# Weight blocks of a two-layer feed-forward stage run ahead by a fifth part, end behind the next functions, and come in another order

## The chip, the cores and the metric

The kernel runs on one NeuronCore of one Trainium2 chip. The metric is the device time of one launch in microseconds (us), the median of several runs. Engines: PE (TensorE, matrix multiply), DVE (VectorE), ACT (ScalarE), POOL (GpSimd), SP (SyncE, which only issues DMAs here).

## The reference, cut to what matters

```
x = attention(q, k, v)                 # 2 x 8 heads, 576 positions, head size 64, with rotary embedding
x = x.reshape(1152, 512)
h = x @ w1_in                          # 512 -> 2048
x = elu(h) @ w1_out                    # 2048 -> 512
h = x @ w2_in                          # 512 -> 2048
out = (h * tanh(softplus(h))) @ w2_out # mish, 2048 -> 512
```

The weights reach the chip as 64-bit floats. Each product is made of three passes on numbers that are split into a high and a low part (hi·hi, hi·lo, lo·hi).

## The kernel before, in words

**Blocks of weights.** Each of the four weight matrices is cut into 16 blocks of 128x512. One block is a *job*: SP loads `raw` (512 KB); POOL makes `wu` from the upper words (L96); DVE adjusts exponent, sign and mantissa in three instructions (L100, L104, L108); and the last step is two instructions, ACT copying `wu` to the high part (L122) and POOL subtracting it to get the low part (L123). `weight_stages` is a generator that yields between these parts. `open_job` starts a job (load and L96), `advance` runs its next part, `weight_part` opens jobs until two run and advances the older, `weight_job` runs parts until one more job is finished. After the opening part a job has four parts: three on DVE and the last step. Tiles are named by matrix side and parity of the group of four blocks: `wi0h`, `wi0l`, `wi1h`, ..., `wo1l`; each name has four buffers.

**The list of jobs.** Jobs 0 to 31 are the first layer's blocks (w1_in and w1_out by turns, in groups of four). Jobs 32 to 63 are the second layer's. Groups 4 to 7 name its four groups. Before, jobs 32 to 47 are: w2_in group 4, w2_in group 5, w2_out group 4, w2_out group 5.

**Steps.** Behind the attention come 64 steps. Step n makes one first product (`g1_mm`, L183: 24 matmuls of 288 columns into a PSUM tile `ps_s`), applies the function to it, issues second products that have become due, and takes up some weight work. Steps 0 to 31 are the first layer: `elu` (ACT L214, L215, L216; DVE L217, L218), `elu_hi` (ACT L223), `elu_lo` (DVE L227), second products `g2_first` (L624: 24 matmuls into `ps_g`). In steps 4 to 30 four weight parts, one job, go into each step: three ahead of `elu`, one behind it. Steps 32 to 63 are the second layer: `mish_a` (ACT L580 tanh and L581 silu straight from `ps_s`, DVE L582), and in batches of two or four steps `mish_b` (ACT L588, after a table load), `mish_c` (ACT L594, after another table load, DVE L595) and `mish_d` (ACT L601, DVE L602); second products `g2_second` (L653: 12 matmuls of 512 columns into `ps_h`), whose first sums into `Y` ACT copies (L657) and whose later ones DVE adds (L659). From step 31 on, each step ends with one `weight_job`, step 36 with two. Of the first layer's last group, four `g2_first` are put off to steps 34, 35, 36 and 38; their results become `XH` (ACT L638) and `XL` (DVE L639).

**What sets the order.** In the first half every engine runs its instructions in the order in which the code writes them. In the second half only ACT does; for the other engines a scheduler decides when the program is built. On the chip each engine runs its own list strictly in order, so an instruction that waits holds back everything behind it on that engine.

**Which step reads what.** Steps 32 to 35 and 40 to 43 read w2_in group 4, steps 36 to 39 and 44 to 47 group 5. The first `g2_second` is due at step 39 and reads w2_out group 4.

Of the kernel before, what the change touches and what calls it, by code (L numbers as in the profile page):

```python
# [13 lines left out]
AF = mybir.ActivationFunctionType  # L14
# [13 lines left out]
def kernel(  # L28
# [11 lines left out]
    nc = tc.nc  # L40
# [10 lines left out]
    GF = 4  # L51
    GB, GE, PB = 9, 2, 5
    NG = NF // GF
# [32 lines left out]
    def weight_stages(key):  # L86
        kind, c = key
        raw = raws.pop(key)
        if wide:


            w = raw.rearrange("p (n w) -> p n w", w=2)
            low, high = w[:, :, 0], w[:, :, 1]
            u = wpool.tile([128, 512], F32, tag="wu", name="wu", bufs=2)
            ui = u.bitcast(I32)
            nc.gpsimd.tensor_scalar(  # L96
                out=u, in0=high.bitcast(F32), scalar1=REBASE, scalar2=0.0, op0=ALU.mult, op1=ALU.add
            )
            yield
            nc.vector.tensor_scalar(  # L100
                out=ui, in0=ui, scalar1=3, scalar2=0x7FFFFFF8, op0=ALU.logical_shift_left, op1=ALU.bitwise_and
            )
            yield
            nc.vector.scalar_tensor_tensor(  # L104
                out=ui, in0=high, scalar=-0x80000000, in1=ui, op0=ALU.bitwise_and, op1=ALU.bitwise_or
            )
            yield
            nc.vector.scalar_tensor_tensor(  # L108
                out=ui, in0=low, scalar=29, in1=ui, op0=ALU.logical_shift_right, op1=ALU.bitwise_or
            )  # L110
            yield
        else:
            u = raw
        even = c // GF % 2 == 0
        pool, tag = wpool if even else late_pool[0], ("wi", "wo")[kind] + ("0" if even else "1")
        hi = pool.tile([128, 512], F32R, tag=tag + "h", name=tag + "h", bufs=GF)
        lo = pool.tile([128, 512], F32R, tag=tag + "l", name=tag + "l", bufs=GF)
        if kind == 0:
            WI[c] = (hi.rearrange("p (c f) -> p c f", c=NC), lo.rearrange("p (c f) -> p c f", c=NC))
        else:  # L120
            WO[c] = (hi, lo)
        nc.scalar.activation(out=hi, in_=u, func=AF.Copy)  # L122
        nc.gpsimd.tensor_tensor(out=lo, in0=u, in1=plain(hi), op=ALU.subtract)  # L123

    jobs = []
    for kind, g in [(k, g) for g in range(NG) for k in range(2)] + [
        (0, NG), (0, NG + 1), (1, NG), (1, NG + 1), (0, NG + 2), (0, NG + 3), (1, NG + 2), (1, NG + 3)
    ]:
        jobs += [(kind, g * GF + i) for i in range(GF)]
    loaded, opened, njob = [0], [0], [0]  # L130
    running = []

    def prefetch_weights(n):
        while loaded[0] < min(len(jobs), opened[0] + n):
            load_weight(jobs[loaded[0]])
            loaded[0] += 1

    def open_job():
        prefetch_weights(3)
        running.append(weight_stages(jobs[opened[0]]))  # L140
        opened[0] += 1
        advance(-1)
        prefetch_weights(3)

    def advance(i):
        if next(running[i], True):
            running.pop(i)
            njob[0] += 1

    def weight_part():  # L150
        while len(running) < 2 and opened[0] < len(jobs):
            open_job()
        if running:
            advance(0)

    def weight_job():
        n = min(njob[0] + 1, len(jobs))
        while njob[0] < n:
            weight_part()
# [35 lines left out]
    def tmp(tag):  # L195
        if tmp_pool[0] is not None:
            return tmp_pool[0].tile([128, S], F32, tag="P", name="P", bufs=PB)
        return late_pool[0].tile([128, S], F32, tag=tag, name=tag, bufs=5)
# [363 lines left out]
    def moe(mp, early):  # L562
# [15 lines left out]
        def mish_a(n, m, f, b, o):  # L578
            t, s = tmp("ta"), tmp("tb")
            nc.scalar.activation(out=v2(t), in_=o[:, :, :HS], func=AF.Tanh, scale=0.5)  # L580
            nc.scalar.activation(out=v2(s), in_=o[:, :, :HS], func=AF.Silu)  # L581
            nc.vector.scalar_tensor_tensor(out=s, in0=t, scalar=-3.0, in1=s, op0=ALU.add, op1=ALU.mult)  # L582
            mst[n] = (m, f, b, t, s)
# [6 lines left out]
        def mish_c(ns):  # L590
            nc.scalar.preload_act_table_set("silu_and_others")
            for n in ns:
                m, f, b, t, s = mst[n]
                nc.scalar.activation(out=t, in_=t, func=AF.Tanh, scale=-1.0)  # L594
                nc.vector.scalar_tensor_tensor(out=s, in0=t, scalar=1.0, in1=s, op0=ALU.add, op1=ALU.mult)  # L595

        def mish_d(ns):
            for n in ns:
                m, f, b, t, s = mst.pop(n)
                gh, gl = galloc(m, f, b)  # L600
                nc.scalar.activation(out=gh, in_=s, func=AF.Copy, scale=-0.25)  # L601
                nc.vector.scalar_tensor_tensor(  # L602
                    out=gl, in0=s, scalar=-0.25, in1=plain(gh), op0=ALU.mult, op1=ALU.subtract
                )
                seam(m, f, b)
# [35 lines left out]
        def g2_second(g, t):  # L641
            o = g_pool[0].tile([128, 512], F32, tag="h", name="ps_h", bufs=2)
            b, s0 = divmod(t * 128, S)
            k = 0
            for fi in range(GF):
                f = NF + g * GF + fi
                hi, lo = WO[f]
                if s0 + 128 <= S:
                    gh, gl = (G[f, b][:, i, s0:s0 + 128] for i in range(2))
                else:  # L650
                    gh, gl = (GX[f][:, i, :] for i in range(2))
                for l, w in ((gh, hi), (gl, hi), (gh, lo)):
                    nc.tensor.matmul(o, lhsT=l, rhs=w, start=(k == 0), stop=(k == 3 * GF - 1))  # L653
                    k += 1
            y = get_y().rearrange("p (t e) -> p t e", e=DM)[:, t, :]
            if g == 0:
                nc.scalar.activation(out=y, in_=o, func=AF.Copy)  # L657
            else:
                nc.vector.tensor_tensor(out=y, in0=y, in1=o, op=ALU.add)  # L659
                if g == NG - 1:  # L660
                    nc.sync.dma_start(out=out[t * 128:t * 128 + 128, :], in_=y)
# [4 lines left out]
        blocks[-4:] = [(1, g, b) for g in range(NG - 2, NG) for b in range(NB)]  # L666
        g1_seq = [(m, g * GF + fi, b) for m, g, b in blocks for fi in range(GF)]
        half = len(g1_seq) // 2
        D1, D2, LATE, XJ = 1, 4, (3, 4, 5, 7), 4
        pend = []  # L670

        def run_g2(it):
# [10 lines left out]
        def step(n, late):  # L683
            m, f, b = g1_seq[n]
            o = early.pop(n) if n in early else g1_mm(m, f, b)
            if late:
                mish_c(late)
            done, late = late, []
            if m == 0:
                for _ in range(3 if GF <= n < half - 1 else 0):  # L690
                    weight_part()
                if o is not None:
                    o = elu(m, f, b, o)
                if GF <= n < half - 1:
                    weight_part()
                if o is not None:
                    o = elu_hi(*o)
            else:
                mish_a(n, m, f, b, o)
                mish_d(done)  # L700
            if f % GF == GF - 1:
                g = f // GF
                if m == 0:
                    pend.extend((n + (D1 if n < half - 1 else LATE[e]), (0, (g, b, e))) for e in range(NC))
                else:
                    pend.extend((n + D2, (1, (g, t))) for t in TB[b])
            if n in batches:
                late = batches[n]
                mish_b(late)
            cnt = 2 if len(pend) > 5 or pend and pend[0][1][0] == 0 and n in (half - 2, half + 6) else 1  # L710
            while pend and cnt and pend[0][0] <= n:
                run_g2(pend.pop(0)[1])
                cnt -= 1
            if m == 0:
                if o is not None:
                    elu_lo(*o)
            for _ in range(0 if n < half - 1 else 1 + (n == half + XJ)):
                weight_job()
            return late

        pools = ExitStack()
# [13 lines left out]
        with tc.manual_schedule(engines=MANUAL):  # L735
            late = []
            for n in range(half, 2 * half):
                if n == half + 7:
                    psum("ps_h")
                    s_more[0] = g_pool[0]  # L740
                    s_count[0] = 0
                late = step(n, late)
            mish_c(late)
            mish_d(late)
            while pend:
                run_g2(pend.pop(0)[1])
# [75 lines left out]
```

## Time and profile before

| | |
|---|---|
| runs of the kernel | 598.58, 599.16, 601.9 us, median 599.16 us |
| the profiled execution | 597.68 us, its span 595.9 us |
| mean granted TensorE clock in it | 0.979 of full speed |
| busy share of the span | PE 96%, DVE 73%, ACT 62%, POOL 42% |
| the first layer's steady steps | about 200 to 370 us of the span |
| the passage from the first to the second layer | about 370 to 422 us |
| the second layer's steady steps | about 422 to 567 us, then the last second products |

The time of an execution is its span and 1.8 us around it. A busy PE is not a PE at its peak: what counts is how long a stretch of known matmuls takes, from the start of its first to the start of what follows.

### The profile page before, as it was taken

What the parts mean: (1) busy time and instruction counts of PE and PEld (TensorE: products, weight loads), DVE (VectorE), ACT (ScalarE), POOL (GpSimd) and SP (SyncE); (2) the same over time, 40 slices, a digit from 0 to 9 for tenths busy, and PEclk for the clock granted to TensorE, in tenths of its full rate; (3) what the DMA queues carried; (4) which work ended last, traced back from release to release, by engine and by line L of the source; (5) the groups of instructions that cost most, each with busy time, mean ns of one, the idle gap of its engine ahead of it and who ended that gap; (6) DMA issues with size and microseconds to landing.
All of it is one profiled execution on the core that took longest, in us unless ns stands there. A gap on an engine that the chain in (4) does not pass through costs nothing.

```text
span 595.9 us, 10312 instructions
## 1 busy us (share of the span) xinstructions
PE 573.3 (96%) x3794; PEld 501.2 (84%) x3794; DVE 437.9 (73%) x740; ACT 371.6 (62%) x637; POOL 251.0 (42%) x226
## 2 busy tenths in 40 slices
PE   7899999988999999999999999997999999999997
PEld 6676666645567999999999999997799898999985
DVE  6878889899925766777777777899588677774552
ACT  3467777766756665554454555883967858578660
POOL 6596867767740224223233232445245253332000
PEclk8789999999999999999999999997999999999999
DMA  6585658926410222222232223233243331300022
GB/s 220 138 243 149 161 143 229 262 72 192 133 37 1 71 90 89 71 96 83 71 100 78 71 74 104 78 109 115 72 127 83 110 101 67 117 19 1 18 89 88
DMA packets 43921, 62.17 MB, mean 104 GB/s; under 512 B 13920, under 2 KB 32096, under 8 KB 43104
## 3 DMA queue, kind: packets, MB, share of 16 engines
q1 hardware_dynamic: 43872, 61.52, 34.6%
q8 instruction: 30, 0.49, 0.3%
q14 instruction: 19, 0.16, 0.1%
HBM read 46.20 MB, written 2.36 MB: 81 GB/s over the span
## 4 chain that ended last, share of the span: by engine, by line
PE 46%; issue 28%; POOL 13%; DVE 10%; DMA 1%; ACT 1%; SPq 0%; POOLq 0%; DVEq 0%; ACTq 0%
PE ps_h L653 16%; PE ps_s L183 13%; PE ps_s L368 7%; PE psA L429 5%; PE psT L408 5%; POOL wu L96 4%; POOL wi1l L123 3%; DVE mn L375 2%; POOL wo0l L123 2%; POOL wo1l L123 2%; POOL wi0l L123 2%; DVE wu L104 2%; DVE P L398 1%; DVE wu L108 1%; DVE wu L100 1%
## 5 line engine op out<-in xcount | busy, mean ns | idle before, releaser
L375 DVE TENSOR_REDUCE mn<-ps_s 128x1 f32<-128x576 f32 x72 | 54.3, 754 | 16.4 <-PE ps_s L368 15.6
L420 ACT ACTIVATE pt<-psT 128x640 f32<-128x640 f32 x64 | 45.0, 703 | 32.6 <-PE psT L408 32.1
L381 ACT ACTIVATE P<-ps_s,mn 128x576 f32<-128x576 f32 x72 | 53.2, 738 | 18.9 <-DVE mn L375 12.0
L123 POOL TENSOR_TENSOR wi1l<-wu,wi1h 128x512 fp32r<-128x512 f32 x16 | 26.1, 1629 | 90.2 <-ACT wi1h L122 90.2
L183 PE MATMUL ps_s<-XH,wi1h 128*128 128x288 f32 x256 | 55.7, 300 | 3.1 <-ACT tb L581 3.0
L408 PE MATMUL psT<-idn,P 128*128 128x128 f32 (+1 forms) x360 | 53.8, 282 | 4.3 <-ACT pt L420 2.7
L183 PE MATMUL ps_s<-XH,wi0h 128*128 128x288 f32 x256 | 55.3, 298 | 0.9 <-DVE tb L218 0.8
L183 PE MATMUL ps_s<-XL,wi1h 128*128 128x288 f32 x256 | 55.9, 300 | 0.0
L100 DVE TENSOR_SCALAR wu<-wu 128x512 int32<-128x512 int32 x64 | 32.8, 512 | 30.8 <-POOL wu L96 30.7
L183 PE MATMUL ps_s<-XH,wi1l 128*128 128x288 f32 x256 | 55.4, 297 | 0.0
L183 PE MATMUL ps_s<-XL,wi0h 128*128 128x288 f32 x256 | 54.8, 296 | 0.0
L183 PE MATMUL ps_s<-XH,wi0l 128*128 128x288 f32 x256 | 54.6, 295 | 0.0
L104 DVE SCALAR_TENSOR_TENSOR wu<-raw,wu 128x512 int32<-128x512 int32 x64 | 53.1, 830 | 1.9
L429 PE MATMUL psA<-pt,v_t 128*64 128x256 f32 (+1 forms) x320 | 53.9, 429 | 0.0
L108 DVE SCALAR_TENSOR_TENSOR wu<-raw,wu 128x512 int32<-128x512 int32 x64 | 50.3, 787 | 1.7
L96 POOL TENSOR_SCALAR wu<-raw 128x512 f32<-128x512 f32 x64 | 48.2, 754 | 5.1
L123 POOL TENSOR_TENSOR wo1l<-wu,wo1h 128x512 fp32r<-128x512 f32 x16 | 24.3, 1518 | 61.6 <-ACT wo1h L122 61.6
L408 PEld LDWEIGHTS psT<-idn,P 128*128 128x128 f32 (+1 forms) x360 | 41.4, 138 | 7.5 <-POOL P L396 2.1
L217 DVE SCALAR_TENSOR_TENSOR tb<-ta,tb 128x576 f32<-128x576 f32 x30 | 22.7, 758 | 32.6 <-ACT tb L216 32.5
L398 DVE TENSOR_SCALAR_CACHE_REDUCE P<-P,rc 128x576 f32<-128x576 f32 x56 | 45.2, 808 | 1.0
L214 ACT ACTIVATE tb<-ps_s 128x576 f32<-128x576 f32 x30 | 19.6, 653 | 41.9 <-PE ps_s L183 41.9
L183 PEld LDWEIGHTS ps_s<-XH,wi1h 128*128 128x128 f32 x256 | 42.2, 192 | 4.1 <-ACT tb L581 3.5
(140 smaller groups left out, 1507.7 us busy)
## 6 DMA issues: line engine op xcount, KB each, us to landing
raw<-in_w_in_dram SPq DMA_DIRECT2D x32, 512.0 KB, 3.7
raw<-in_w_out_dram SPq DMA_DIRECT2D x32, 512.0 KB, 3.3
qk_t<-in_qk_dram SPq DMA_DIRECT2D x6, 1152.0 KB, 7.3
qa<-qh SPq DMA_DIRECT2D x28, 144.0 KB, 5.9
v_t<-in_vp_dram SPq DMA_DIRECT2D x8, 320.0 KB, 3.2
out_dram<-Y SPq DMA_DIRECT2D x9, 256.0 KB, 2.0
ka<-kh SPq DMA_DIRECT2D x14, 144.0 KB, 6.7
ka<-kl SPq DMA_DIRECT2D x14, 144.0 KB, 6.5
```

Source lines behind the costliest of these rows:

```text
L96: nc.gpsimd.tensor_scalar(out=u, in0=high.bitcast(F32), scalar1=REBASE, scalar2=0.0, op0=ALU.mult, op1=ALU.add)
L104: nc.vector.scalar_tensor_tensor(out=ui, in0=high, scalar=-0x80000000, in1=ui, op0=ALU.bitwise_and, op1=ALU.bitwise_or)
L108: nc.vector.scalar_tensor_tensor(out=ui, in0=low, scalar=29, in1=ui, op0=ALU.logical_shift_right, op1=ALU.bitwise_or)
L123: nc.gpsimd.tensor_tensor(out=lo, in0=u, in1=plain(hi), op=ALU.subtract)
L183: nc.tensor.matmul(o[:, j, :HS], lhsT=w[:, cc, :], rhs=x[:, b, cc, j * HS:j * HS + HS], start=(k == 0), stop=(k == 3 * NC - 1),)
L375: nc.vector.tensor_reduce(out=m, in_=psS[u][:, :, :HS], axis=AX.XY, op=ALU.min)
L381: nc.scalar.activation(out=P.rearrange("p (j n) -> p j n", j=2), in_=psS.pop(u)[:, :, :HS], func=AF.Exp, scale=-1.0, bias=mn_t.pop(u), acc ...
L398: eng.tensor_scalar(out=P, in0=P, scalar1=r, scalar2=None, op0=ALU.mult, op1=ALU.add, accum_out=row_sum)
L408: nc.tensor.transpose(tv[:w, c, :], P[:, c * 128:c * 128 + w], idn)
L420: nc.scalar.activation(out=o, in_=tv, func=AF.Copy)
L429: nc.tensor.matmul(o[64 * h:64 * h + 64, :n], lhsT=v_t[p][:, c, 64 * h:64 * h + 64], rhs=pt_t[p, g][:, h, c, :], start=(c == 0), stop=(c = ...
L653: nc.tensor.matmul(o, lhsT=l, rhs=w, start=(k == 0), stop=(k == 3 * GF - 1))
```

## The change

Four things are changed. The jobs of the second layer are listed with w2_out group 4 ahead of w2_in group 5. In steps 8 to 23 two weight parts stand behind `elu` instead of one, five a step instead of four; and at step 31 the jobs that run are finished. From step 33 on (none in steps 32 and 34) a step opens one job and runs its three DVE parts, and the last step waits for the next step, where it stands behind `mish_a`. The first `g2_second` sums are copied to `Y` by DVE instead of ACT.

```
-        (0, NG), (0, NG + 1), (1, NG), (1, NG + 1), (0, NG + 2), (0, NG + 3), (1, NG + 2), (1, NG + 3)
+        (0, NG), (1, NG), (0, NG + 1), (1, NG + 1), (0, NG + 2), (0, NG + 3), (1, NG + 2), (1, NG + 3)
...
+    held = [0]
+
+    def finish_held():
+        while held[0]:
+            advance(0)
+            held[0] -= 1
+
+    def hold_job():
+        open_job()
+        for _ in range(3):
+            advance(-1)
+        held[0] += 1
...
             if g == 0:
-                nc.scalar.activation(out=y, in_=o, func=AF.Copy)
+                nc.vector.tensor_copy(out=y, in_=o)
...
-        D1, D2, LATE, XJ = 1, 4, (3, 4, 5, 7), 4
+        D1, D2, LATE, LATER = 1, 4, (3, 4, 5, 7), {0: 0, 2: 0}
...
-                if GF <= n < half - 1:
+                for _ in range((1 + (8 <= n < 24)) if GF <= n < half - 1 else 0):
                     weight_part()
...
                 mish_a(n, m, f, b, o)
+                finish_held()
                 mish_d(done)
...
-            for _ in range(0 if n < half - 1 else 1 + (n == half + XJ)):
-                weight_job()
+            if n == half - 1:
+                while running:
+                    advance(0)
+            for _ in range(LATER.get(n - half, 1) if n >= half else 0):
+                if opened[0] < len(jobs):
+                    hold_job()
```

After the change line numbers are 13 higher from L183 on (L183 is L196, L580 is L593, L581 is L594, L594 is L607, L653 is L666); L96 to L123 keep theirs, and the new copy is L670.

ACT, before, steps 36 to 38 (L580 and L581 are the functions of one step each, L122 the high part of a weight block):

```order
L594 ACTIVATE ta<-ta 128x576 x2
L580 ACTIVATE ta<-ps_s 128x576
L581 ACTIVATE tb<-ps_s 128x576
L601 ACTIVATE g<-tb 128x576 x2
L638 ACTIVATE XH<-Y 128x576
L122 ACTIVATE wo0h<-wu 128x512 x2
L580 ACTIVATE ta<-ps_s 128x576
L581 ACTIVATE tb<-ps_s 128x576
L122 ACTIVATE wo0h<-wu 128x512
L580 ACTIVATE ta<-ps_s 128x576
L581 ACTIVATE tb<-ps_s 128x576
```

The same steps on ACT after the change:

```order
L593 ACTIVATE ta<-ps_s 128x576
L594 ACTIVATE tb<-ps_s 128x576
L122 ACTIVATE wi1h<-wu 128x512
L614 ACTIVATE g<-tb 128x576 x2
L651 ACTIVATE XH<-Y 128x576
L593 ACTIVATE ta<-ps_s 128x576
L594 ACTIVATE tb<-ps_s 128x576
L122 ACTIVATE wi1h<-wu 128x512
L593 ACTIVATE ta<-ps_s 128x576
L594 ACTIVATE tb<-ps_s 128x576
L122 ACTIVATE wi1h<-wu 128x512
```

Two blocks of w2_out stood ahead of step 37's functions; now each step's functions come first and one block of w2_in group 5 follows them.

PE after the change, from the end of step 37's first product to the start of step 39's, with step 38's shown by its first and last row (`wi1h`, `wi1l` are w2_in group 5, L637 is L624 of before):

```order
L196 MATMUL ps_s<-XH,wi1l 128x288 x2
L637 MATMUL ps_g<-ge,wo1h 128x288 x3
L637 MATMUL ps_g<-ge,wo1l 128x288 x2
L637 MATMUL ps_g<-g,wo1h 128x288 x4
L637 MATMUL ps_g<-g,wo1l 128x288 x2
L637 MATMUL ps_g<-g,wo1h 128x288 x3
L196 MATMUL ps_s<-XH,wi1h 128x288 x2
...
L196 MATMUL ps_s<-XH,wi1l 128x288 x2
L637 MATMUL ps_g<-g,wo1h 128x288
L637 MATMUL ps_g<-g,wo1l 128x288 x2
L637 MATMUL ps_g<-g,wo1h 128x288 x4
L637 MATMUL ps_g<-g,wo1l 128x288 x2
```

Before, the first products of steps 37 and 38 stood back to back and the last `g2_first` in one piece behind them; now 1 of its 24 matmuls stands ahead of step 37's product, 14 between those of steps 37 and 38 and 9 between those of steps 38 and 39.

DVE after the change, one of the steps that take five parts (L230, L231 and L240 are L217, L218 and L227 of before; before, L100, L104 and L108 stood in one run behind L227 and nothing between L218 and L227):

```order
L231 TENSOR_TENSOR tb<-tb,ps_s 128x576
L108 SCALAR_TENSOR_TENSOR wu<-raw,wu 128x512
L240 TENSOR_TENSOR g<-tb,g 128x576
L100 TENSOR_SCALAR wu<-wu 128x512
L104 SCALAR_TENSOR_TENSOR wu<-raw,wu 128x512
L108 SCALAR_TENSOR_TENSOR wu<-raw,wu 128x512
L230 SCALAR_TENSOR_TENSOR tb<-ta,tb 128x576
```

Weight parts now also stand between the two halves of the function, one or two of them.

## Rows read from the trace of the kernel before

**Rows 1.** Busy time by stage: stretch, length, PE, PEld, DVE, ACT, POOL, clock, DMA.

```profile
250.00:275.00 25.00, 25.00 (x192) 25.00 (x191) 18.84 (x28) 12.84 (x20) 7.64 (x9) 1.00 0.26 87
...
400.00:425.00 25.00, 20.48 (x114) 18.49 (x113) 19.28 (x25) 14.65 (x23) 10.85 (x9) 0.86 0.37 122
425.00:450.00 25.00, 25.00 (x151) 22.74 (x150) 19.18 (x27) 19.59 (x31) 10.56 (x10) 1.00 0.33 96
```

**Rows 2.** The chain that ended last: start, length, work.

```profile
425.10 5.60 PE ps_h L653 x24
...
567.63 24.55 PE ps_h L653 x108
```

**Rows 3.** Timeline of PE, 389 to 422 us: start, length, instruction [idle before].

```profile
389.03 0.43 PE L183 MATMUL ps_s<-XH,wi1h 128*128 128x288 f32 x2
...
392.21 0.69 PE L624 MATMUL ps_g<-ge,wo1h 128*128 128x288 f32 x4
...
395.34 0.42 PE L183 MATMUL ps_s<-XH,wi1h 128*128 128x288 f32 x2
...
408.35 0.85 PE L183 MATMUL ps_s<-XH,wi1h 128*128 128x288 f32 x2 [3.02 <-ACT tb L581]
...
414.19 0.62 PE L653 MATMUL ps_h<-wo0h,g 128*128 128x512 f32 x2
...
418.68 0.50 PE L653 MATMUL ps_h<-wo0l,g 128*128 128x512 f32 x1 [1.15 <-POOL wo0l L123]
...
421.81 0.42 PE L183 MATMUL ps_s<-XH,wi0h 128*128 128x288 f32 x2
```

**Rows 4.** Stretches of 2 us in the passage, columns as in rows 1.

```profile
406.00:408.00 2.00, 0.00 (x0) 0.00 (x0) 1.93 (x4) 1.41 (x3) 0.71 (x2) 0.81 0.21 57
408.00:410.00 2.00, 1.65 (x7) 1.65 (x8) 1.44 (x2) 0.97 (x3) 1.74 (x2) 0.50 0.52 205
...
414.00:416.00 2.00, 2.00 (x11) 1.69 (x10) 2.00 (x4) 0.46 (x1) 0.00 (x0) 0.98 0.46 147
```

**Rows 5.** Timeline of ACT, 382 to 407 us.

```profile
382.62 0.78 ACT L588 ACTIVATE ta<-ta,half_col 128x576 f32<-128x576 f32 x1 [2.01 <-DVE tb L582]
...
386.39 0.63 ACT L580 ACTIVATE ta<-ps_s 128x576 f32<-128x576 f32 x1
...
397.50 0.63 ACT L580 ACTIVATE ta<-ps_s 128x576 f32<-128x576 f32 x1
398.03 0.64 ACT L581 ACTIVATE tb<-ps_s 128x576 f32<-128x576 f32 x1
...
402.37 0.62 ACT L122 ACTIVATE wo0h<-wu 128x512 fp32r<-128x512 f32 x1
406.59 0.63 ACT L122 ACTIVATE wo0h<-wu 128x512 fp32r<-128x512 f32 x1 [3.61 <-DVE wu L108]
```

**Rows 6.** Timeline of DVE, the wait ahead of step 33's product.

```profile
379.36 1.50 DVE L100 TENSOR_SCALAR wu<-wu 128x512 int32<-128x512 int32 x1 [1.92 <-POOL wu L96]
```

**Rows 7.** Timeline of POOL, three low parts in the passage.

```profile
376.76 1.84 POOL L123 TENSOR_TENSOR wi1l<-wu,wi1h 128x512 fp32r<-128x512 f32 x1 [11.58 <-ACT wi1h L122]
...
379.29 1.29 POOL L123 TENSOR_TENSOR wi0l<-wu,wi0h 128x512 fp32r<-128x512 f32 x1
...
390.18 3.81 POOL L123 TENSOR_TENSOR wi1l<-wu,wi1h 128x512 fp32r<-128x512 f32 x1 [3.70 <-ACT wi1h L122]
```

**Rows 8.** Timeline of one steady step of the first layer.

```profile
265.12 0.65 ACT L214 ACTIVATE tb<-ps_s 128x576 f32<-128x576 f32 x1 [1.87 <-PE ps_s L183]
...
269.62 0.89 DVE L227 TENSOR_TENSOR g<-tb,g 128x576 fp32r<-128x576 f32 x1
...
271.27 0.69 PE L624 MATMUL ps_g<-g,wo1h 128*128 128x288 f32 x4
```

**Rows 9.** PE in the attention: a stretch (columns as in rows 1) and a wait.

```profile
136.00:140.00 4.00, 2.10 (x13) 1.26 (x13) 3.90 (x10) 3.17 (x7) 2.98 (x3) 1.00 0.71 238
...
137.58 0.53 PE L368 MATMUL ps_s<-ka,qa 128*128 128x288 f32 x2 [1.58 <-ACT P L381]
```

More of the change, by code (lines that the diff above doesn't have):

```diff
@@ L743, in moe @@
             mish_c(late)
+            finish_held()
             mish_d(late)
```

## The prediction

> **What bounds the kernel now.** I read the stages first. In the steady steps of the first layer PE is busy for all of the stretch, in the second layer's too; between them, in the passage, it falls to 20.48 of 25 us and its clock to 0.86 [rows 1]. The chain of waits agrees: behind the passage it holds PE alone, to the last products [rows 2]. So what the passage loses goes into the end one for one, and in the steady steps time on another engine costs nothing while PE doesn't wait for it.
>
> The size of that loss comes from PE's timeline. From the end of step 36's first product to the start of step 40's it runs from 392.21 to 421.81, 29.60 us [rows 3]. The work in it is three first products (3.18 us each: 389.03 to 392.21), two `g2_first` (3.13 each: 392.21 to 395.34) and two `g2_second` (5.60 for both [rows 2]): 9.54 + 6.26 + 5.60 = 21.40 us. **The loss is 8.2 us.** It has three parts. Step 39's product waits 3.02 us for a silu of ACT (3.3 us counted from start to start, with two tenths more ahead of step 38's). It then takes 5.84 us instead of 3.18, 2.66 too many, because the clock has fallen to 1.2 GHz, 0.50 in its rows, and rises to 2.4 GHz as it ends [rows 4]. And the first `g2_second` takes 7.62 with its neighbour instead of 5.60, waiting for high and low parts of w2_out group 4 [rows 3].
>
> Why was ACT late? At 402.37 it makes the high part of one w2_out block, and the next such copy stands in front of step 37's functions and waits 3.61 us for DVE [rows 5]. The functions behind it hold PE's `ps_s`.
>
> **The change part by part.**
>
> *Another order and fifth parts.* In steps 8 to 23 there are 16 more parts, four jobs. Jobs 8 to 38 are done at the end of step 30 and job 39 at step 31, so all of w2_out group 4 is ready long before step 39. That removes 2.02 us at the `g2_second`.
>
> The price is DVE and ACT work in the steady steps: in 25 us DVE has 18.84 us of work, ACT 12.84, POOL 7.64 [rows 1]. A quarter more weight work cannot fill them. What counts is lateness: ACT starts a step's function at 265.12, the low part is done at 269.62 + 0.89 = 270.5, and the second product that reads it starts at 271.27 but comes to it only with its last 6 of 24 matmuls, 2.4 us on, at 273.6 [rows 8]. The cover is 3.1 us. One L122 (0.62) and its wait ahead of L214, and two DVE parts between the halves, delay it by about 2 us. I cost this at nothing; without the cover it would be some 0.2 us in each of 16 steps, 3 us. Buffers don't stop it either: job 36 writes where group 2 of w1_out lay, last read in step 27, and it finishes in step 28.
>
> *The last step behind the functions.* Step 37's functions no longer wait for DVE, so the 3.3 us wait and its fall of the clock lose their cause. But a new wait arises. Of w2_in group 5, jobs 41, 42 and 43 now end in steps 36, 37 and 38, each behind the functions of that step, and are read by the very next first product. So PE waits for: first product done, tanh, silu, high copy, and then POOL's low part.
>
> ACT issues tanh, silu and copy 0.53 us apart [rows 5]; the copy takes 0.62. With three handovers of some 0.05 the high part is there 1.77 us after PE's recorded end, which lies 0.16 behind the point where its next matmul may start: 1.93 us on PE's own count. PE's cover is what stands between: 14 matmuls of 0.13 (1.84 us) ahead of step 38, 9 (1.18) ahead of step 39. Waits for the high part: 0.1 and 0.75 us.
>
> For step 37 ACT's backlog decides. It comes to step 36 at 397.50 now. Ahead of that stand two last steps instead of five (three times 0.57, so 1.7), and the wait of 2.01 us [rows 5] shrinks by about 1.1 since DVE's L100, which it was behind [rows 6], now waits for POOL without a later collision. ACT arrives at about 394.7, the copy is readable at 396.5; PE is there at 395.34 + 0.13 = 395.47. Wait: 1.05 us (0.8 to 1.3).
>
> Then the low parts. PE has 4 matmuls on the high part (0.53 us) while POOL works. The trace has this subtraction between 1.29 us and 3.81 us [rows 7]. In all three places ACT's copy meets a DVE instruction that is about to end, followed by one that reads PSUM or itself waits; that is nearest to the row of 1.29, with a short wait: I take 1.4, and with handovers PE waits 1.0 us, three times, 3.0 us.
>
> On the ports the row of 3.81 starts while DVE runs a chain of instructions. The Trainium skill (SBUF — State Buffer, SBUF: two separate sides) states that the port pair which VectorE and GpSimd share is an exclusive lock: a DVE instruction with two SBUF inputs that starts first blocks a GpSimd instruction until it ends. By that rule each low part here waits for at most the rest of one DVE instruction and the sum stays as it is; by the longest row alone it would be the slower rival below.
>
> *Copies on DVE.* Nine copies of 128x512 leave ACT and come to DVE. In the second layer's steady steps DVE has 19.18 of 25 us [rows 1], PE none to spare; the first two sums are copied before the tile is needed again, one first product later (3.18 us). Nothing. Nor does the DMA order matter: the same blocks are loaded.
>
> *The sum.* New waits: 1.05 + 0.1 + 0.75 + 3.0 = 4.9 us. Old loss: 8.2 us. Change: -3.3 us. The profiled execution of 597.68 (its span 595.9 and 1.8 around it) would be 594.4. It stands 1.5 us below the median of 599.16, so the median forecast is 599.16 - 3.3 = **595.9 us**.
>
> **The rivals.**
>
> *A: as summed*, 595.1 to 596.7: 45%.
>
> *B: the new waits hardly bind.* ACT reaches step 36 another 1 us earlier and POOL takes 1.29 at once, or PE's cover is larger than the modelled ends let it seem: 1 to 3 us left of the 4.9. The change is -5.2 to -7.2: 592.0 to 594.0. For it: the wait chain is made of short handovers that may overlap. Against it: 14 and 9 matmuls of cover are fixed by the order. 20%.
>
> *C: the clock falls again.* Around step 37 PE would wait 1.05 and then 1.0 us with 0.53 of work between. Before, the clock fell after one wait of 3.02 [rows 3, 4]; in the attention 1.58 of waiting in a stretch with 2.10 of 4 us busy left it at 1.00 [rows 9]. The new place lies between the two. The price is what one fall cost, 2.66 us: 599.16 - 3.3 + 2.7 = 598.6. 20%. The Trainium skill (TensorE: Matmul & The Clock Gate, Part 1) says that the clock follows how busy the engine has been recently, so two near waits may count together; by that rule this rival is possible though no single wait is as long as 3.02, and no row here shows such a pair.
>
> *D: the fifth part stalls PE* in steps 8 to 23 by 0.2 us each, 3.2 in all: 599.1. Against it stands the cover of 3.1 us [rows 8]. 7%.
>
> *E, the other side: POOL is held as in the row of 3.81.* If all three low parts in steps 36 to 38 take 3.81 instead of 1.4, PE waits 3 x 2.4 = 7.2 us more: 599.16 - 3.3 + 7.2 = 603.1. It decides from a mean of 2.5 us per low part on, where the gain is used up. One of the three rows shown is of that size [rows 7], but behind a chain of DVE work that the new order doesn't have there. 8%.
>
> **How the numbers follow.** A measurement here tells about 0.5% from no change, 3.0 us: faster means below 596.2, slower above 602.2. Of A some six tenths lie below (27%), all of B (20%): 47%, taken as 0.48. The rest of A, C and D: 0.44. E: 0.08. The range leaves out E and the lower part of B: 592.8 to 599.4.
>
> **What would show it.** After the change the wait of 3.02 us for a silu ahead of step 39 and the ones for `wo0h` and `wo0l` in the first `g2_second` are gone; instead PE waits ahead of `wi1h` and `wi1l` in steps 37, 38 and 39, for ACT L122 and POOL L123, about 2, 1.1 and 1.75 us; the clock stays at 1.00 in the passage; the steady stretches keep PE busy throughout [rows 1]. From step 36's first product to step 40's the 29.60 become 26.3. The prediction is wrong if PE idles in steps 8 to 23, if the clock is below 1 in the passage, or if L123 there lasts well over 1.8.

## The result and the profile after

The changed kernel takes **607.41 us** (median of 4 runs, 606.96 to 607.94) against 599.61 us for the kernel before in the same series (its three runs listed further up, and a fourth of 600.05): a ratio of 1.0125, 95% interval [1.0094, 1.0157]. It is slower by 7.8 us; the forecast was 595.9 with a range up to 599.4. The profiled execution took 607.1 us, its span 605.3, 9.4 more than before.

Stages of the changed kernel first (stretch, length, PE, PEld, DVE, ACT, POOL, clock, DMA):

```profile
250.00:275.00 25.00, 24.98 (x190) 24.75 (x188) 19.40 (x29) 10.38 (x17) 8.35 (x8) 1.00 0.23 85
275.00:300.00 25.00, 22.79 (x169) 22.56 (x170) 18.84 (x28) 12.83 (x21) 9.51 (x9) 1.00 0.32 100
300.00:325.00 25.00, 22.13 (x154) 21.67 (x153) 18.62 (x27) 10.81 (x17) 9.35 (x10) 0.93 0.27 91
400.00:425.00 25.00, 21.32 (x141) 19.98 (x140) 17.00 (x26) 12.99 (x20) 6.33 (x6) 0.93 0.23 74
```

The passage (400 to 425) looks better than in [rows 1]: 21.32 against 20.48 us busy, the clock 0.93 against 0.86. The passage itself now lies some 10 us later, so the two stretches don't hold the same steps; its length from start to start, further down, is the fair measure. But the first layer's steady stretch, where PE had been busy for all of 25 us, now idles. The chain still ends in PE alone:

```profile
577.06 24.54 PE ps_h L666 x108
```

The last second products take what they took in [rows 2], and start 9.4 us later.

All waits of PE between 268 and 340 us (start, length, instruction [idle before]):

```profile
276.35 0.53 PE L637 MATMUL ps_g<-g,wo1h 128*128 128x288 f32 x2 [1.37 <-ACT g L236]
277.74 0.54 PE L637 MATMUL ps_g<-g,wo1h 128*128 128x288 f32 x2 [0.87 <-DVE g L240]
305.21 0.53 PE L637 MATMUL ps_g<-ge,wo0h 128*128 128x288 f32 x2 [2.00 <-ACT ge L236]
306.61 0.84 PE L637 MATMUL ps_g<-ge,wo0h 128*128 128x288 f32 x2 [0.87 <-DVE ge L240]
334.20 0.53 PE L637 MATMUL ps_g<-g,wo0h 128*128 128x288 f32 x2 [0.63 <-ACT g L236]
335.60 0.54 PE L637 MATMUL ps_g<-g,wo0h 128*128 128x288 f32 x2 [0.87 <-DVE g L240]
```

They stand in pairs, in steps 16, 20 and 24, always at the second product that is first to read a group of four finished functions: it waits for the last function's high part (L236), then its low part (L240). From the start of one first product to that of the next these steps take 9.13, 10.23 (and 7.40 in step 21) and 8.37 us instead of 6.3 to 6.4. From the start of step 8 to that of step 30 it is 149.26 us (218.61 to 367.87) against 139.43 before (217.45 to 356.88): **+9.83**.

Why the functions are late is seen on ACT (its L122 and L227 rows from 263 to 293 us, and the L236 that stands right behind a copy):

```profile
263.52 0.63 ACT L122 ACTIVATE wi0h<-wu 128x512 fp32r<-128x512 f32 x1 [2.31 <-DVE wu L108]
264.05 0.63 ACT L227 ACTIVATE tb<-ps_s 128x576 f32<-128x576 f32 x1
...
269.14 0.63 ACT L122 ACTIVATE wo0h<-wu 128x512 fp32r<-128x512 f32 x1 [0.64 <-DVE wu L108]
269.67 0.64 ACT L227 ACTIVATE tb<-ps_s 128x576 f32<-128x576 f32 x1
...
275.09 0.63 ACT L122 ACTIVATE wo0h<-wu 128x512 fp32r<-128x512 f32 x1 [3.34 <-DVE wu L108]
275.63 0.67 ACT L236 ACTIVATE g<-tb 128x576 fp32r<-128x576 f32 x1
276.20 0.63 ACT L227 ACTIVATE tb<-ps_s 128x576 f32<-128x576 f32 x1
...
279.98 0.63 ACT L122 ACTIVATE wo0h<-wu 128x512 fp32r<-128x512 f32 x1 [1.72 <-DVE wu L108]
...
284.98 0.63 ACT L122 ACTIVATE wo0h<-wu 128x512 fp32r<-128x512 f32 x1 [2.78 <-DVE wu L108]
285.51 0.64 ACT L227 ACTIVATE tb<-ps_s 128x576 f32<-128x576 f32 x1
...
292.33 0.63 ACT L122 ACTIVATE wi1h<-wu 128x512 fp32r<-128x512 f32 x1 [2.37 <-DVE wu L108]
292.86 0.63 ACT L227 ACTIVATE tb<-ps_s 128x576 f32<-128x576 f32 x1
```

The copy of a block stands in front of the function (L227) or, at 275.09 and 279.98, between its parts, and there ACT waits for DVE's L108. Before, in [rows 8], L214 waited for nothing but PE. In four steps L227 comes 28.81 us later (264.05 to 292.86), 7.20 a step, while PE's work in four steps, at 6.3 to 6.4 each, is 25.4. DVE, in turn, makes that L108 behind the function of the step:

```profile
273.70 0.75 DVE L231 TENSOR_TENSOR tb<-tb,ps_s 128x576 f32<-128x576 f32 x1
274.37 0.69 DVE L108 SCALAR_TENSOR_TENSOR wu<-raw,wu 128x512 int32<-128x512 int32 x1
...
276.32 1.36 DVE L240 TENSOR_TENSOR g<-tb,g 128x576 fp32r<-128x576 f32 x1 [0.60 <-ACT g L236]
```

The sum into `Y` (L647; L634 before the change) stands between the two halves of the function in both kernels; the list of DVE's order in the part on the change leaves it out.

So a late function makes the next L108 late, that the next copy, and that the next function. In step 15, the last of its group, the low part is done at 276.32 + 1.36 = 277.7, 11.4 us behind its first product's end at 266.24. Before it was 5.4 (265.08 to 270.5 in [rows 8]). From step 8 to step 15 of the changed kernel this distance is 5.5, 6.5, 7.1, 8.0, 7.6, 9.3, 10.5 and 11.4 us: it grows in all but one of these steps.

In the passage PE shows these rows (first rows of step 36's and step 40's products, and all waits between):

```profile
399.94 0.43 PE L196 MATMUL ps_s<-XH,wi1h 128*128 128x288 f32 x2
...
407.75 0.53 PE L196 MATMUL ps_s<-XH,wi1h 128*128 128x288 f32 x2 [1.22 <-ACT wi1h L122]
409.18 0.85 PE L196 MATMUL ps_s<-XH,wi1l 128*128 128x288 f32 x2 [0.62 <-POOL wi1l L123]
...
416.76 0.54 PE L196 MATMUL ps_s<-XH,wi1l 128*128 128x288 f32 x2 [0.61 <-POOL wi1l L123]
...
421.48 0.53 PE L196 MATMUL ps_s<-XH,wi1h 128*128 128x288 f32 x2 [0.61 <-ACT wi1h L122]
422.89 0.54 PE L196 MATMUL ps_s<-XH,wi1l 128*128 128x288 f32 x2 [0.62 <-POOL wi1l L123]
...
431.24 0.42 PE L196 MATMUL ps_s<-XH,wi0h 128*128 128x288 f32 x2
```

The waits of [rows 3] for a silu and for w2_out are gone; the five new ones stand where the prediction put them (the sixth, for the high part ahead of step 38, doesn't show). The stretch takes 31.30 us instead of 32.78. It also contains one of two falls of the clock (stretches of 2 us):

```profile
306.00:308.00 2.00, 1.39 (x6) 1.39 (x7) 1.97 (x3) 1.09 (x2) 1.06 (x1) 0.66 0.26 104
308.00:310.00 2.00, 2.00 (x10) 2.00 (x10) 1.86 (x4) 0.63 (x1) 0.37 (x1) 0.50 0.07 10
...
408.00:410.00 2.00, 1.38 (x7) 1.14 (x7) 2.00 (x3) 1.42 (x3) 1.91 (x2) 0.76 0.00 0
410.00:412.00 2.00, 2.00 (x11) 2.00 (x10) 1.97 (x4) 0.00 (x0) 0.25 (x1) 0.50 0.15 33
```

The account of the 9.4 us: +9.83 in steps 8 to 30, -0.08 from there to step 36, -1.48 in the passage, and +1.16 ahead of step 8 (218.61 against 217.45), where nothing was changed; the profiles of the kernels below, whose code is the same there, start step 8 between 216.68 and 218.57.

### The profile page after: what moved, and what is told of

Same layout as the page of the kernel before. It is cut to its first block, busy times and chain, and to the rows that moved or that the text cites. A ratio compares the mean times of both kernels' runs of the same rounds, so it can differ in the third digit from the quotient of the medians.

```text
span 605.3 us, 10313 instructions
## 1 busy us (share of the span) xinstructions
PE 577.9 (95%) x3794; PEld 503.4 (83%) x3794; DVE 452.3 (75%) x749; ACT 366.6 (61%) x628; POOL 242.4 (40%) x226
## 4 chain that ended last, share of the span: by engine, by line
PE 46%; issue 30%; POOL 13%; DVE 8%; DMA 1%; ACT 1%; SPq 0%; POOLq 0%; DVEq 0%; ACTq 0%
PE ps_h L666 16%; PE ps_s L196 13%; PE ps_s L381 7%; PE psA L442 5%; PE psT L421 5%; POOL wu L96 5%; POOL wi1l L123 3%; POOL wo0l L123 2%; DVE mn L388 2%; POOL wo1l L123 2%; POOL wi0l L123 2%; DVE P L411 1%; DVE wu L104 1%; DVE wu L108 1%; DMA qk_t<-in_qk_dram 1%
## 5 line engine op out<-in xcount | busy, mean ns | idle before, releaser
L123 POOL TENSOR_TENSOR wi1l<-wu,wi1h 128x512 fp32r<-128x512 f32 x16 | 21.5, 1341 | 95.1 <-ACT wi1h L122 87.7
L196 PE MATMUL ps_s<-XH,wi1l 128*128 128x288 f32 x256 | 55.4, 297 | 1.9 <-POOL wi1l L123 1.9
L196 PE MATMUL ps_s<-XH,wi1h 128*128 128x288 f32 x256 | 55.2, 297 | 1.8 <-ACT wi1h L122 1.8
L196 PE MATMUL ps_s<-XH,wi0h 128*128 128x288 f32 x256 | 55.8, 300 | 0.9 <-DVE tb L231 0.8
L593 ACT ACTIVATE ta<-ps_s 128x576 f32<-128x576 f32 x32 | 20.6, 645 | 57.7 <-PE ps_s L196 57.7
L196 PE MATMUL ps_s<-XL,wi1h 128*128 128x288 f32 x256 | 55.3, 297 | 0.0
L196 PE MATMUL ps_s<-XL,wi0h 128*128 128x288 f32 x256 | 55.2, 298 | 0.0
L196 PE MATMUL ps_s<-XH,wi0l 128*128 128x288 f32 x256 | 54.8, 296 | 0.0
L104 DVE SCALAR_TENSOR_TENSOR wu<-raw,wu 128x512 int32<-128x512 int32 x64 | 51.9, 811 | 1.7
L108 DVE SCALAR_TENSOR_TENSOR wu<-raw,wu 128x512 int32<-128x512 int32 x64 | 51.8, 809 | 1.6
L96 POOL TENSOR_SCALAR wu<-raw 128x512 f32<-128x512 f32 x64 | 50.1, 785 | 5.1
L100 DVE TENSOR_SCALAR wu<-wu 128x512 int32<-128x512 int32 x64 | 36.7, 574 | 15.1 <-POOL wu L96 15.0
L123 POOL TENSOR_TENSOR wo1l<-wu,wo1h 128x512 fp32r<-128x512 f32 x16 | 21.5, 1344 | 64.3 <-ACT wo1h L122 64.3
L230 DVE SCALAR_TENSOR_TENSOR tb<-ta,tb 128x576 f32<-128x576 f32 x30 | 23.1, 768 | 29.4 <-ACT tb L229 29.2
L196 PEld LDWEIGHTS ps_s<-XH,wi0h 128*128 128x128 f32 x256 | 41.8, 190 | 3.6 <-issue 1.3
```

Source lines behind the costliest of these rows:

```text
L96: nc.gpsimd.tensor_scalar(out=u, in0=high.bitcast(F32), scalar1=REBASE, scalar2=0.0, op0=ALU.mult, op1=ALU.add)
L104: nc.vector.scalar_tensor_tensor(out=ui, in0=high, scalar=-0x80000000, in1=ui, op0=ALU.bitwise_and, op1=ALU.bitwise_or)
L108: nc.vector.scalar_tensor_tensor(out=ui, in0=low, scalar=29, in1=ui, op0=ALU.logical_shift_right, op1=ALU.bitwise_or)
L196: nc.tensor.matmul(o[:, j, :HS], lhsT=w[:, cc, :], rhs=x[:, b, cc, j * HS:j * HS + HS], start=(k == 0), stop=(k == 3 * NC - 1),)
```

## The experiments

For each run: the median, its ratio to the kernel before in the same series, and from its trace the length of steps 8 to 30 (start to start) and of the passage (start of step 36's product to that of step 40's). Without a loss the passage would take four products, two `g2_first` and two `g2_second`: 12.72 + 6.26 + 5.60 = 24.58 us by [rows 2, 3].

| kernel | median us | ratio [95%] | steps 8 to 30 | passage |
|---|---|---|---|---|
| before | 599.61 | 1 | 139.43 | 32.78 |
| changed | 607.41 | 1.0125 [1.0094, 1.0157] | 149.26 | 31.30 |
| e1_dve_ahead | 595.56 | 0.9912 [0.9887, 0.9936] | 139.44 | 29.71 |
| e2_act_late | 598.28 | 0.9975 [0.9955, 0.9995] | 142.40 | 29.74 |
| e4_copy_alone | 599.25 | 0.9978 [0.9957, 1.0] | 139.44 | 35.12 |
| e5_no_skip | 591.02 | 0.9847 [0.9823, 0.987] | 139.44 | 25.31 |
| e6_fifth_to_27 | 589.62 | 0.9821 [0.9796, 0.9846] | 139.43 | 24.59 |
| e7_no_hold | 594.78 | 0.9911 [0.9875, 0.9946] | 139.43 | 28.86 |
| e8_act_copy | 594.81 | 0.9916 [0.9886, 0.9946] | 139.43 | 29.82 |
| e9_shift1 | 620.36 | 1.0345 [1.0305, 1.0386] | 154.42 | 33.06 |
| e10_shift2 | 610.67 | 1.0189 [1.0149, 1.0228] | 145.50 | 33.51 |
| e11_shift3 | 601.16 | 1.0024 [1.0003, 1.0045] | 139.44 | 34.26 |
| e12_early_no_hold | 590.17 | 0.986 [0.9822, 0.9897] | 139.44 | 24.59 |

### Where the five parts stand: e1 and e2

Both keep all that the change does, five parts a step in steps 8 to 23 too, and move parts within the step. In e1 all DVE parts stand ahead of `elu` (four, in every fourth step three), and last steps that are due stand behind `elu`, as before the change:

```
+                mid = 8 <= n < 24
+                if mid:
+                    for _ in range(3 + (n % 4 > 0)):
+                        dve_part()        # L100, L104 or L108 of the oldest job that has one left
...
                 if o is not None:
                     o = elu(m, f, b, o)
+                if mid:
+                    last_steps()          # L122, L123 of the jobs whose DVE parts are issued
```

In e2 DVE's order is word for word that of the changed kernel; only ACT's and POOL's last steps go behind `elu_hi` of their step.

> The changed kernel with the weight work of steps 8 to 23 placed otherwise: only DVE parts ahead of the function (3 in every fourth step, 4 in the others), and the last step (ACT copy, POOL subtraction) of each block whose DVE parts are done between L216 and L223's place, as before the change. The amount of work is the same. Theory 1 (ACT's copy waits for a DVE part of the same step and holds the function behind it) and theory 2 (DVE parts between the halves of the function make it late): PE's 9.7 us of longer steps vanish, 597.7 us, some 9.5 below the changed kernel. Theory 3 (a quarter more weight work is too much for DVE, POOL and their shared port, wherever it stands): the stalls stay, 605 to 608.

> The changed kernel with DVE's and PE's lists as they are; only the last steps of steps 8 to 23 are put behind L223 of their step on ACT (POOL follows). Theory 1: the stalls of steps 8 to 23 vanish, 597.7 us. Theory 2: they stay, 604 to 608, since DVE's order is the same. Theory 3: they stay.

e1 removes the whole loss: no wait of PE in steps 8 to 30, and 595.56 us, 2.1 below what was expected. DVE is busy for 21.59 of the 25 us from 250 on and PE for all of them. e2 removes 6.9 of the 9.8 us, so of its theories neither the first nor the second holds alone; what is left are these waits:

```profile
300.70 0.53 PE L655 MATMUL ps_g<-ge,wo0h 128*128 128x288 f32 x2 [0.63 <-DVE ge L258]
...
326.86 0.54 PE L655 MATMUL ps_g<-g,wo0h 128*128 128x288 f32 x2 [0.73 <-ACT g L254]
328.08 0.54 PE L655 MATMUL ps_g<-g,wo0h 128*128 128x288 f32 x2 [0.68 <-DVE g L258]
```

The amount of work is the same in all three kernels, so the amount isn't the cause. The places are: 6.9 us go when ACT's copies leave their places ahead of or inside a function, and the other 3.0 when DVE's parts leave theirs between its halves too, as in e1 (where the copies also stand a little earlier than in e2). The five waits of the passage are in e1 as in the changed kernel, 1.11 us and four times 0.61, of which these are the first two:

```profile
397.86 0.54 PE L212 MATMUL ps_s<-XH,wi1h 128*128 128x288 f32 x2 [1.11 <-ACT wi1h L122]
399.28 0.53 PE L212 MATMUL ps_s<-XH,wi1l 128*128 128x288 f32 x2 [0.61 <-POOL wi1l L123]
```

Its passage loses 29.71 - 24.58 = 5.13 us, and the clock stays at 1.00 in it:

```profile
398.00:400.00 2.00, 1.39 (x9) 1.15 (x10) 2.00 (x4) 1.52 (x3) 1.91 (x2) 1.00 0.00 0
```

### The copies alone: e4 and e8

e4 is the kernel before with nothing but the copies of the first sums moved to DVE; e8 is e1 with these copies back on ACT.

```
-                nc.scalar.activation(out=y, in_=o, func=AF.Copy)
+                nc.vector.tensor_copy(out=y, in_=o)
```

> The kernel before with the first sums of the second layer copied by DVE as the only change. PE is never waiting there: 599.6 us, within 1 us. If the copies hold DVE up in front of the functions of the second layer, 601 to 603.

> Base: e1. Edit: the first second-layer sums are copied by ACT again, as before the change. Theory 1 (the copies lie beside PE's work on either engine, as in e4): 594.6 to 596.6, no measurable difference from e1. Theory 2 (the copies on ACT stand in front of a function or a last step when the passage is tight): 1 us or more slower than e1, with a wait for ACT around step 40.

Neither is measurably slower or faster than its base: 599.25 us beside a median of 600.21 for before in that series, and 594.81 beside e1's 595.56. As far as the times tell, the copies lie beside PE's work on either engine, as costed.

The passage of e4's trace is 35.12 us long all the same, 2.34 more than before's. PE waits for the same silu:

```profile
407.57 0.54 PE L183 MATMUL ps_s<-XH,wi1h 128*128 128x288 f32 x2 [3.02 <-ACT tb L581]
...
415.99 0.99 PE L653 MATMUL ps_h<-wo0h,g 128*128 128x512 f32 x2 [2.88 <-ACT wo0h L122]
```

But the clock stays at 1.00 behind that wait:

```profile
408.00:410.00 2.00, 2.00 (x17) 2.00 (x16) 1.46 (x3) 1.45 (x3) 1.71 (x2) 1.00 0.46 129
```

PE is through step 39's product sooner than in [rows 3], then waits 2.88 us for `wo0h` (0.36 in before's trace), and the clock falls to 0.50 behind this second wait instead. So the 2.66 us that the fall cost in before's trace didn't lie on top of the wait for w2_out: without the fall that wait was longer. One trace of each doesn't show whether the copies have to do with where the clock falls.

The fifth part alone, with the old list of jobs, was expected at 604 to 609 us, but that program ends in a deadlock and has no time. In the old list job 36, which the fifth parts bring into step 28, is a block of w2_in group 5 and writes where steps 28 to 31 still read; that this is the cause is argued and not shown. The new list without fifth parts has no run either, so no run separates the order of the jobs from the number of blocks done early.

### The blocks that end one step ahead of their reader: e5, e6, e7, e12

All four stand on e1. e5 lets steps 32 and 34 hold a block too (`LATER = {}`), e6 goes on with fifth parts to step 27 (`mid = 8 <= n < 28`), and e7 holds nothing: the last step stands at the end of the step that opened its block, ahead of the next functions. e12 is e6 with nothing held.

```
     def hold_job():
         open_job()
-        for _ in range(3):
+        for _ in range(4):
             advance(-1)
-        held[0] += 1
```

> Base: the version of e1 (595.56 us), where DVE's parts stand ahead of the function and the last steps behind its ACT part. Edit: steps 32 and 34 open and hold a job too, so the blocks of w2_in group 5 end two steps earlier (jobs 41 to 43 in steps 34 to 36). Theory 1 (the five waits for L122 and L123 in steps 36 to 39, 4.05 us in e1, stand there only because each block ends in the step ahead of the one that reads it): they vanish in part or whole, and the time falls by 2 to 4 us to 591.5 to 593.5. Theory 2 (ACT and POOL are the bound of the passage: what ends earlier in one place delays the functions in another): a new wait for a function of steps 34 to 36 comes, and the time is 595 to 599.

> Base: e1. Edit: the fifth part goes into steps 8 to 27 instead of 8 to 23, so one more job is done ahead of the passage and each block of w2_in group 5 ends one step earlier against its reader. Theory 1 (the place of the parts, not their number, made the stalls of the changed kernel): no step of the first layer is longer than 6.5 us, the waits in steps 37 to 39 shrink by 2 us or more, 592 to 594. Theory 2 (a fifth part costs by its amount of work): four more steps of it add stalls in steps 24 to 27 and the time is 596 or more.

> Base: e1. Edit: nothing is held; the last step of a block stands at the end of the step that opened it, ahead of the next step's functions, as before the change. Theory 1 (standing behind the functions is what removed the 3.02 us wait for a silu): ACT waits for DVE L108 ahead of tanh and silu again, PE waits 1 to 3 us for a function in one or more of steps 37 to 39, perhaps with a fall of the clock: 597 to 601. Theory 2 (the order of the jobs alone removed it, since fewer blocks end in the passage): 594 to 596.5, the same as e1 or faster, because the blocks of w2_in group 5 are ready earlier.

> Base: the version with fifth parts in steps 8 to 27, DVE's parts ahead and the last steps behind the function (589.62 us, no wait from step 8 on). Edit: no block is held; its last step stands at the end of the step that opened it, ahead of the next functions. Theory 1 (with one block more done early, the order and the places in the first layer are all that is needed): 588.5 to 591, no wait of PE above 0.5 us in the passage. Theory 2 (holding is needed once the other waits are gone, because ACT waits for DVE ahead of the functions): a wait for a function of 0.5 to 2 us in the passage, 590.5 to 594.

In e5 (591.02 us, 0.5 below the range of its first theory) the five waits have become one, for a silu:

```profile
399.50 0.53 PE L212 MATMUL ps_s<-XH,wi1h 128*128 128x288 f32 x2 [0.45 <-ACT tb L610]
```

In e6 none is left. The stretch that had held 20.48 us of PE's work now holds 25:

```profile
400.00:425.00 25.00, 25.00 (x155) 22.82 (x154) 21.49 (x30) 16.34 (x26) 9.24 (x8) 1.00 0.30 90
```

e6 is the fastest of all: 589.62 us, 1.8% below before and 2.9% below the changed kernel (589.62 / 607.41). That is 2.4 us below the range expected, since all of the waits went and not 2 us of them. Four more steps of five parts cost nothing, 139.43 us. That is the second time that the number of parts is shown to be harmless.

e7 decides for its second theory in the time: 594.78 us, e1's within the intervals. Neither tanh nor silu waits for DVE in the passage, and PE waits twice only, for the high and the low part of one block; the copy of that block stands on ACT behind the making of `XH`, which waits 2.58 us for DVE:

```profile
401.17 0.53 PE L211 MATMUL ps_s<-XH,wi1h 128*128 128x288 f32 x2 [1.59 <-ACT wi1h L122]
402.58 0.53 PE L211 MATMUL ps_s<-XH,wi1l 128*128 128x288 f32 x2 [0.62 <-POOL wi1l L123]
```

There the clock falls (stretches of 2 us):

```profile
402.00:404.00 2.00, 1.42 (x7) 1.42 (x8) 0.70 (x1) 0.71 (x2) 1.91 (x3) 0.76 0.00 0
404.00:406.00 2.00, 2.00 (x11) 2.00 (x10) 2.00 (x3) 0.00 (x0) 1.22 (x2) 0.50 0.00 0
```

e12 says the same without that fall: 590.17 us, no wait in the passage. So the other list of jobs with enough blocks done early removes the silu wait; the last step behind the functions is not needed for it. (e7's four runs lie at 593.2 and 596.3 us, two each; its trace is of one at 593.21.)

### One turn of the parts and nothing else: e9, e10, e11

These test the cause in the kernel before, without more work in the steady steps. In step 8 one, two or three parts more are issued, once. From step 9 on each step has its four parts again, turned by as many places.

```
-                if GF <= n < half - 1:
+                for _ in range(1 + 1 * (n == 8) if GF <= n < half - 1 else 0):
                     weight_part()
```

(2 and 3 times in e10 and e11.)

> Base: the kernel before. Edit: step 8 takes one weight part more, once; every later step still takes four. So from step 9 to 30 the parts stand turned by one: L104, L108 and the last step ahead of the function, L100 between its halves. Theory 1 (a loop through two in-order engines carries lateness on): L108 ends, ACT copies, then makes the function, DVE its two instructions, L100, the sum into Y, the low part, L104 and the next L108. From starts of rows that loop is .69 + .72 + .71 + .87 + .67 + .40 + .67 + .67 + .72 + .72 + .53 = 7.4 us, against 6.35 us of PE's work a step. The function comes 1.0 us later each step until PE waits (low part about 11 us behind the product instead of 5.4, some 6 steps); then each step takes 7.4: 599.5 + 22 x 1.0 - 5.6 = about 616, 610 to 622. Theory 2 (each step by itself, as the prediction had it: a delay under the cover): 598 to 602. Theory 3 (the amount of weight work): the same amount, 598 to 602.

> As the run with one part more, but two parts more in step 8: from step 9 on L108, the last step and L100 stand ahead of the function, L104 between its halves. Theory 1: the loop is without one L100 and one L104 behind the low part, .69 + .72 + .71 + .87 + .67 + .64 + .67 + .67 + .72 + .53 = 6.9 us, 0.5 more than PE's step: 599.5 + 22 x 0.5 - 5.6 = about 605, 600 to 608. Theories 2 and 3: 598 to 602.

> As the run with one part more, but three parts more in step 8: from step 9 on the last step, L100 and L104 stand ahead of the function and L108 between its halves. Theory 1: L108 is done before the low part of the step, so ACT's copy ahead of the next function never waits, and the loop is 4.9 us, less than PE's step; no lateness grows: 598.5 to 601, no difference from before, with a function that starts 0.5 us late (the copy ahead of it) in each step or not at all. Theory 2: the same. A rival to both (any part between the halves of the function costs by itself): 602 or more.

ACT in e9, its copies from 256 to 271 us:

```profile
256.13 0.63 ACT L122 ACTIVATE wi0h<-wu 128x512 fp32r<-128x512 f32 x1 [2.31 <-DVE wu L108]
...
263.42 0.64 ACT L122 ACTIVATE wi0h<-wu 128x512 fp32r<-128x512 f32 x1 [2.31 <-DVE wu L108]
...
270.71 0.63 ACT L122 ACTIVATE wi0h<-wu 128x512 fp32r<-128x512 f32 x1 [2.31 <-DVE wu L108]
```

And in e10, from 254 to 269 us:

```profile
254.37 0.63 ACT L122 ACTIVATE wi0h<-wu 128x512 fp32r<-128x512 f32 x1 [1.85 <-DVE wu L108]
...
261.20 0.64 ACT L122 ACTIVATE wi0h<-wu 128x512 fp32r<-128x512 f32 x1 [1.85 <-DVE wu L108]
...
268.04 0.63 ACT L122 ACTIVATE wi0h<-wu 128x512 fp32r<-128x512 f32 x1 [1.85 <-DVE wu L108]
```

The copies come every 7.29 us in e9 and every 6.83 or 6.84 in e10, while PE's step is 6.35. The loops summed beforehand were 7.4 and 6.9. In e11 the copy is ready and waits for nothing, and the function waits for PE again:

```profile
250.96 0.63 ACT L122 ACTIVATE wi0h<-wu 128x512 fp32r<-128x512 f32 x1
252.91 0.65 ACT L214 ACTIVATE tb<-ps_s 128x576 f32<-128x576 f32 x1 [1.31 <-PE ps_s L183]
```

One part more, once in 22 steps, thus makes the kernel 3.4% slower; three parts more make it at most half a per cent slower. Steps 8 to 30 grow by 14.99, 6.07 and 0.01 us. The first two fit a lateness of 0.94 and 0.49 us a step over the 19 steps 9 to 27 (27 is the last step of the last group that PE needs in that stretch), less the cover of 3.1 us: 17.9 - 3.1 = 14.8 and 9.3 - 3.1 = 6.2. The 5.6 us of cover in the expectations were read from where PE had waited in the changed kernel; the 3.1 of the prediction, counted at the groups' ends, fits better, but that was seen afterwards, and so was the count of 19 steps in place of 22. In the whole, e9 lies in its range, e10 is 2.7 us above the upper end of its range and e11 0.2 above its own. Behind step 30 lie 9.0 of the 23.8 us by which e9's trace is longer than before's, 7.8 of e10's 14.6, and in e11 3.6 us; no expectation had costed these stretches, so that e9's total came out in its range is in part luck. What these three runs show of the loop are the lengths of steps 8 to 30.

## Why the prediction was wrong

**The step that failed** is the price of the fifth parts: "One L122 (0.62) and its wait ahead of L214, and two DVE parts between the halves, delay it by about 2 us. I cost this at nothing". The delay was taken for one step, as if each began on time. The cover of 3.1 us that it was set against fits: the delay in step 15 is 11.4 - 5.4 = 6.0 us, since it had grown over the steps from 8 on, 6.0 - 3.1 = 2.9, and step 16 is 9.13 - 6.37 = 2.76 us too long. ACT's copy waits for DVE's L108, DVE's next L108 stands behind instructions that wait for ACT's function, and that loop takes longer than PE's step: in the changed kernel 7.20 us in the mean of the four steps shown and 7.1 from step 8 to step 22, in e9, where one turn is held all along, 7.29. e1 and e11, where the loop is cut, lose nothing in steps 8 to 30. So the term of the sum that was put at nothing measured 9.83 us. Of the three signs of being wrong that the prediction names, two came: PE idles in steps 8 to 23, and the clock falls in the passage.

**Rival D** had the right place (PE idles in steps 8 to 23) and the wrong size: 0.2 us in each of 16 steps, 3.2 in all. It came in a few large pieces, 9.83 us, because only the last function of a group of four is awaited. Two neighbouring waits, 2.00 and 0.87, were also followed by a fall of the clock there.

**"A quarter more weight work cannot fill them"** held: e1 and e6 do it at 139.44 and 139.43 us for steps 8 to 30.

**The passage.** "That removes 2.02 us at the `g2_second`" and the end of the 3.02 us wait came true. The new waits were forecast as 4.9 us in steps 37 to 39. In e1, where the clock stays up, the passage loses 5.13. Term by term the high parts cost 1.11, nothing and 0.61 us by their rows (forecast 1.05, 0.1 and 0.75) and the low parts 0.61 each (forecast 1.0). From start to start it is more: in the two rows of e1 399.28 - 397.86 - 0.53 of work is 0.89 for the first low part. In the prediction's own terms tanh, silu, copy and three handovers add up to 1.83 us and not to 1.77, about 0.1 us in the whole. So in e1 this part of the forecast holds; in the changed kernel itself the gain is 1.48 us, and the fall of the clock accounts for most of what is missing. The gain of e1 in the passage is 32.78 - 29.71 = 3.07 against the forecast 3.3. Its median gains 4.7 us, more than its trace shows, because the profiled execution of before lies 2.5 us below the median of that series.

**POOL's low part** took 1.34 us at 407.78 in the changed kernel and 1.32 to 1.35 in the other three of w2_in group 5, against the 1.4 chosen from [rows 7]; rival E falls. The rule of the Trainium skill (SBUF — State Buffer, SBUF: two separate sides), that the port pair of VectorE and GpSimd is an exclusive lock, was read as a short wait here, and these rows agree with that.

**Rival C**, the clock, happened in the changed kernel's passage: behind 1.22 and 0.62 us of waiting it fell to 0.50. Between it and e1, with the same order, lie 31.30 - 29.71 = 1.59 us (0.11 of them in the longer first wait), less than the 2.66 that was taken over from before.

**The last step behind the functions** was argued to be what frees step 37's functions. e7 and e12 don't bear that out: the list of jobs and the blocks done early do it, and no run separates these two.

**What stays open** is when the clock falls. Waits of 1.22 and 0.62 in the changed kernel's passage and of 1.59 and 0.62 in e7 were followed by a fall; 1.11 and 0.61 in e1 and 1.23 and 0.61 in e8 were not. The single wait of 3.02 us was followed by a fall in before and not in e4, so the lengths of the waits alone don't tell. That the clock follows how busy the engine has lately been (the Trainium skill, TensorE: Matmul & The Clock Gate, Part 1) speaks for counting neighbouring waits together, but doesn't separate the changed kernel from e8.

## What to carry to other kernels

When two engines run strictly in order and each waits for the other once in a step, add up the loop (here copy, function, exponent work, next copy) and compare it with the bounding engine's step, before a delay is set against a cover. Below the step's length a delay heals by the next step; above it, each step adds the difference, and the cover only says when that is first seen. Busy shares don't show this: ACT was busy for 10.38 to 12.83 of 25 us when it set the pace.

If a count of parts per step is changed, look where every part then stands in each of the steps until the pattern repeats. A count that is no multiple of a job's parts turns the pattern from step to step (five against four: by one place), and one of those places may be the one that closes the loop.

## What the runs showed that was not expected

A block whose copy stands behind the functions was expected to hold PE less than one ahead of them. With enough blocks done early it made no difference (589.62 and 590.17 us). And the whole loss of the passage, 8.2 us by the prediction's count, could be removed by work done earlier: its length of 24.59 us in e6 is the 24.58 of the bare products.
